# Gated linear attention and a bilinear feed-forward on one core: seven input loads move to ScalarE's own hardware queue, and seven filling matmuls run ahead of the first sums

## The chip, the cores and the metric

The kernel runs on one core of one Trainium2 chip. The metric is the device time of one execution in microseconds (us). Of each kernel there are a few timed runs and one profiled execution with its trace; times inside the kernel are counted from the start of the profiled span. The engines are called as the profile calls them: PE (matmuls; PEld loads its weights), DVE (VectorE), ACT (ScalarE), POOL (GpSimd) and SP (SyncE). A "q" behind a name (SPq, ACTq, PEq) is the sequencer of that engine, which issues DMAs and waits on semaphores.

## The reference, cut to what is computed

```
# q, k, v, alpha: (B, H, S, D) = (4, 8, 768, 48); moe_w_a, moe_w_b: (384, 1536); moe_w_out: (1536, 384)
for t in range(S):
    state = alpha[:, :, t, :, None] * state + einsum('bhd,bhe->bhde', k[:, :, t], v[:, :, t])
    y[:, :, t] = einsum('bhd,bhde->bhe', q[:, :, t], state)
x = y.transpose(0, 2, 1, 3).reshape(B * S, H * D)
out = ((x @ w_a) * (x @ w_b)) @ w_out
```

A recurrence with one decay per token, head and channel gives y; each token's eight heads side by side are a row of 384 numbers; and a feed-forward layer multiplies two projections to 1536 channels with each other and projects back to 384.

## The kernel before, in words

**Chunks.** The work is cut into six chunks. Chunk c holds 256 tokens (the third c // 2 of the sequence) of two of the four batches (c % 2 tells which two). Its loads `ld a`, `ld q`, `ld k`, `ld v` (function `load`, line 404) bring alpha, q, k and v of both batches into tiles of 128 partitions; each partition gets two neighbouring tokens of every head, so every contiguous run in HBM is 384 bytes. A load of a, q or k for a whole chunk is 768 KB of float32, one of v is cast to bfloat16 on its way. The tiles of a, q and k have two buffers each, so a load for chunk c can only start when the readers of chunk c - 2 are done.

**Attention of one chunk.** ACT takes logarithms of alpha (`ln`, line 411), PE sums them along the tokens (`B` line 453, `A2` line 503, `AQ` line 498), ACT makes exponentials of the sums (`E`, line 532: `beta` and `invb`). POOL or DVE multiplies one of the two tokens of each pair of q and k by a ratio, in place (`lv`, level, line 517; for q it reads `ra`, which ACT makes at line 510). DVE multiplies k by invb (`mk`) and q by beta (`mq`) into `QKp` (line 543). `QKp` is turned into `kqT`, in chunks 0 and 1 by PE, later by a DMA transpose that SP issues (`T`, line 595). PE makes scores (`D`, line 665), which are masked by DVE (`M`, line 670) or copied by ACT (`Mc`, line 674) and masked in place by DVE (`Mm`, line 678). `KA` and `K` (line 618) update the running state, `SA`, `SB` (line 694) and `Y` (line 715) add up y, `X` (lines 755 and 757) takes it out of PSUM on ACT or DVE, and `XT` (line 762) turns it by a DMA transpose that SP issues, into `xT`.

**Feed-forward of one chunk.** For each of the twelve blocks f of 128 channels PE computes `a f` and `b f` from xT (line 777, three matmuls each, of 512 tokens), ACT copies the a part out (`as f`, line 783), and DVE multiplies it with the b part into `prod` (`pr f`, line 791). Then `o m 0` and `o m 1` (line 799, six matmuls each, over f 0 to 5 and 6 to 11) project 128 tokens back; `ot` (lines 814, 816) copies the result out, and `st` (line 832) stores it.

**Order.** All of it stands in one hand-written list, `PROGRAM` (lines 17 to 258). An entry `3: ld k * P` means: of chunk 3, load k of both batches (`*`), issued from POOL (`P`; `S` is ACT, `V` is DVE, `Y` is SP). The number behind `a`, `b`, `D`, `o` and others is the PSUM bank, of eight. The list is walked once, and each engine executes its own instructions in the order of the list; engines wait for each other on semaphores only. So an engine that has little to do, such as POOL, gets ahead of the others in the list until one of its instructions has to wait. The attention of chunk c + 1 and c + 2 is woven between the feed-forward matmuls of chunk c.

**The places that the change touches.** At the head: `c1a` (line 325) loads ACT's table, `c1` (`const_fill`, line 327) sets on DVE the tile `wz` of zeros and two small constants, `fill n i` (line 435) runs n matmuls of wz with itself, 128 x 512, into bank i; their results are never read. Before the change, `c1` stands behind `Bs 0b`, and there are two fills: `fill 5 2` and `fill 1 1`. Along the way: the loads `4: ld a` (line 97), `3: ld k` (147), `4: ld q` (150), `5: ld a` (157), `4: ld k` (177), `5: ld k` (184) and `5: ld q` (215). Their first users:

- `3: ld k` is followed in its own entry by `lv 0 k P; lv 1 k P`; two entries on stand `mk 0 V; mq 0 V` of the same chunk, and then `2: a 1 * 2; b 5 * 0; as 5 *; pr 5 *`. A later `2: a 7 * 0` uses bank 0 again, which `pr 5` has to free.
- `5: ld a` is first read by `5: ln *` (line 166), behind which ACT has `as 11`, `ot 1`, `as 6` and `as 8` of the same stage; the `a 6 * 5` there uses the bank that `as 11` frees.
- `4: ld k` is followed at once by `lv 1 k V; lv 0 k V`, and DVE has `3: X 1 V` behind them (line 182), whose `XT 1` gives the last part of chunk 3's xT.
- `5: ld q` is followed by `lv 1 q P`; `lv 0 q V` (line 225) stands on DVE ahead of `3: pr 7` (line 226), which `3: o 2 1` needs.

Of the kernel before, what the change touches and what calls it, by code (L numbers as in the profile page):

```python
# [14 lines left out]


PROGRAM = """
0: c1a; cz 0 q V; cz 0 b P; cs 0 m P; ci; cz 1 q V; cz 0 v V; ld a 0b Y; ln 0b; cs 0 0 P; cm 0; cu; cu2 P; B 0b 3; Bs 0b; c1; cs 1 m P; ld v 0 P; ld a 1 P
0: cz 1 b P; ld a 0a Y; ln 0a; B 0a 1; Bs 0a; E 0a b; fill 5 2; cus; ld q 0a Y; mq 0a V; E 0b i; ld q 0b Y; ld k 0a Y; ld k 0b Y; mk 0b V; E 0b b; mq 0b V
0: C 0 1 5; E 0a i; mk 0a V; Ce 0 1 V; C 0 0 3; Ce 0 0 V; dk 0 6; fill 1 1; v 0 S; de 0; K 0 0 7; k 0 0 V; ln 1; cs 1 0 P; ld q 1 P; ld k 1 P; W b 0 256  # L20
0: cm 1; ld v 1 P; c2 P; c3 P; D 0 1 5; M 0 1; D 0 0 0; SB 0 6; B 1a 4; Bs 1a; Mc 0 0; Mm 0 0 V; B 1b 5; Bs 1b; E 1a i; E 1a b; mq 1a V; mk 1a V; K 0 1 4; E 1b i
# [72 lines left out]
1: pr 10 0; b 0 0 1; a 3 0 4; as 0 0; pr 0 0  # L94
2: lv 1 k P; mk 1 V
1: as 3 0; b 3 0 7; a 1 0 6; as 1 0
4: ld a * P
1: b 7 0 0; b 1 0 4; pr 1 0; as 7 0; pr 7 0; pr 3 0
2: mk 0 V
1: SB 1 0  # L100
3: ln *
1: a 6 0 2; as 6 0; b 9 0 3; a 4 0 5; a 9 0 6; as 9 0; pr 9 0
2: mq 1 V; T 1
0: o 2 0 4
# [39 lines left out]
2: a 5 * 6; b 4 * 3  # L144
3: E 1 i
1: st 0 Y
3: dr; ld k * P; lv 0 k P; lv 1 k P
4: lx V; R 0
3: mk 0 V; mq 0 V; T 0
4: ld q * Y  # L150
2: a 1 * 2; b 5 * 0; as 5 *; pr 5 *
4: ra 1
2: b 7 * 4; b 10 * 1; pr 4 *; a 10 * 6; as 10 *; pr 10 *
3: mk 1 V
2: a 7 * 0; b 1 * 5; a 0 * 6; b 0 * 7; as 1 *; as 7 *; pr 1 *; pr 7 *; as 0 *; a 3 * 0; b 9 * 1; pr 0 *
3: mq 1 V; ld v * P
5: ld a * P
2: as 3 *; b 3 * 2; a 9 * 6
4: ra 0
2: pr 3 *; as 9 *; pr 9 *; a 2 * 5  # L160
4: lv 0 q P
2: as 2 *; b 2 * 7; pr 2 *
3: KA * 06; D 0 0 4; M 0 0; dl; k * 0 V; k * 1 V
# [10 lines left out]
4: lv 1 q V  # L174
3: SB 1 4; D 1 1 0; Mc 1 1; Mm 1 1 V; SA 0; Y 0; X 0 S; XT 0
2: o 0 0 2
4: ld k * P; lv 1 k V; lv 0 k V
2: o 0 1 -
4: AQ 6; E 0 i
2: ot 0 S  # L180
4: E 0 b
3: SA 1; Y 1; X 1 V; XT 1
4: E 1 i; E 1 b; mk 1 V
5: ld k * P; lv 1 k P
2: o 2 0 1; o 2 1 -; o 3 0 6; o 1 0 0; o 3 1 -; o 1 1 -
4: dr
1: st 1 Y
# [24 lines left out]
4: SB 0 3; SB 1 5; D 1 1 0; Mc 1 1  # L212
3: b 3 * 7; pr 3 *; b 10 * 2
4: D 1 0 0; Mc 1 0; Mm 1 1 V
5: ld q * P; lv 1 q P
3: pr 10 *
4: SA 1; SA 0; Y 0; X 0 S; XT 0
3: o 2 0 7; o 1 0 1
# [737 lines left out]
```

## Time and profile before

| | us |
|---|---|
| median of 3 runs | 205.07 |
| lowest and highest of them | 195.19 and 207.42 |
| the profiled execution's own time | 196.55 |
| its span, first to last instruction | 194.8 |
| PE busy | 183.4 (94%) |
| DVE busy | 137.2 (70%) |
| ACT busy | 103.0 (53%) |
| POOL busy | 55.8 (29%) |

The span is the time from the first to the last instruction of the profiled execution; 1.75 us of its own time lie around it. Busy time of PE is that of overlapping matmuls, whose ends are modelled. The idle time of an engine counts only where another one waits for it in the end. The profile has a chain of waits: the work that ended last, followed back from the last instruction, at each step to whatever released it. A timeline row has the start, the time taken, the engine, the line, the operation, output and inputs, how many instructions were merged, and, in brackets, how long the engine had been idle and what ended that. For DMAs "to landing" is the time from the issue to the last byte's arrival.

### The profile page before, as it was taken

How to read it: one execution, taken by the hardware profiler on the slowest of the kernel's cores; microseconds unless marked ns; L12 is line 12 of the kernel's file. 1: busy time of each engine (PE TensorE's matmuls, PEld its weight loads, DVE VectorE, ACT ScalarE, POOL GpSimd, SP SyncE). 2: the span in 40 equal slices, each digit the busy share in tenths (PEclk: the TensorE clock that was granted, in tenths of full speed). 3: DMA queues.
4: the chain of work that ended last, by engine and by line, in shares of the span. 5: the costliest groups of instructions: out<-in, count | busy, mean ns of one | idle time of the engine just before them, and what ended most of it. 6: DMA issues, size and time to landing. Idle time of an engine off the chain costs nothing.

```text
span 194.8 us, 5851 instructions
## 1 busy us (share of the span) xinstructions
PE 183.4 (94%) x2498; PEld 111.5 (57%) x2498; DVE 137.2 (70%) x230; ACT 103.0 (53%) x189; POOL 55.8 (29%) x75
## 2 busy tenths in 40 slices
PE   1998899899999999999998989999999999999993
PEld 1577675566687877644555534555544556544463
DVE  3588966999899796779979379786755871147520
ACT  4465766686765668555566035766245712154401
POOL 8999734860640424400512400040000000000000
PEclk9999999999999999999999999999999999999999
DMA  5999999999999997999996996566388005013013
GB/s 127 263 214 188 237 231 257 245 247 258 255 228 232 189 252 142 127 267 226 131 237 131 131 277 150 111 51 78 82 156 183 3 3 112 9 43 121 2 40 122
DMA packets 57882, 30.96 MB, mean 159 GB/s; under 512 B 47824, under 2 KB 54880, under 8 KB 57856
## 3 DMA queue, kind: packets, MB, share of 16 engines
q0 software_dynamic: 19680, 18.09, 49.0%
q1 hardware_dynamic: 38032, 12.41, 31.5%
q8 instruction: 19, 0.31, 0.6%
q10 hardware_dynamic: 144, 0.10, 0.2%
q14 instruction: 7, 0.06, 0.1%
HBM read 25.98 MB, written 4.74 MB: 158 GB/s over the span
## 4 chain that ended last, share of the span: by engine, by line
PE 75%; DMA 10%; POOL 8%; issue 2%; DVE 2%; ACT 2%; POOLq 0%; ACTq 0%; DVEq 0%
PE psum L777 43%; PE psum L799 20%; DMA wb_t<-in_moe_w_b_dram 7%; DMA xT<-ys 3%; PE psum L665 3%; PE psum L715 2%; PE psum L618 2%; DVE prod L791 1%; POOL a_t L404 1%; PE psum L498 1%; PE psum L689 1%; PE psum L694 1%; POOL wa_t L384 1%; PE psum L810 1%; POOL v_t L404 1%
## 5 line engine op out<-in xcount | busy, mean ns | idle before, releaser
L777 PE MATMUL psum<-xT,wb_t 128*128 128x512 bf16 (+1 forms) x270 | 57.1, 337 | 0.8 <-DVE prod L791 0.3
L777 PE MATMUL psum<-xT,wa_t 128*128 128x512 bf16 (+1 forms) x270 | 56.1, 337 | 0.7 <-DMA xT<-ys 0.7
L799 PE MATMUL psum<-wo_t,prod 128*128 128x384 bf16 x276 | 48.5, 326 | 0.7 <-issue 0.7
L777 PEld LDWEIGHTS <-wb_t 128*128 128x128 bf16 x270 | 25.6, 98 | 21.6 <-issue 1.1
L777 PEld LDWEIGHTS <-wa_t 128*128 128x128 bf16 x270 | 25.4, 98 | 20.5 <-issue 1.2
L799 PEld LDWEIGHTS <-prod 128*128 128x128 bf16 x276 | 26.2, 98 | 17.6 <-issue 0.7
L517 POOL TENSOR_TENSOR q_t<-q_t,ra 128x384 f32<-128x384 f32 x8 | 9.1, 1135 | 46.8 <-ACT ra L510 32.0
L674 ACT ACTIVATE m<-psum 128x1024 bf16<-128x1024 f32 x16 | 16.2, 1022 | 6.3 <-PE psum L665 6.3
L816 DVE COPY ot<-psum 128x384 f32<-128x384 f32 (+1 forms) x13 | 6.9, 538 | 16.5 <-PE psum L799 14.1
L814 ACT ACTIVATE ot<-psum 128x384 f32<-128x384 f32 (+1 forms) x12 | 5.7, 477 | 12.9 <-PE psum L799 11.9
L678 DVE TENSOR_TENSOR m<-m,mask 128x1024 bf16<-128x1024 bf16 x16 | 11.6, 732 | 0.4 <-ACT m L674 0.4
L543 DVE TENSOR_TENSOR QKp<-k_t,invb 128x768 bf16<-128x768 f32 x10 | 11.1, 1114 | 0.2
L411 ACT ACTIVATE la<-a_t 128x1536 f32<-128x1536 f32 (+2 forms) x9 | 9.5, 1057 | 3.2 <-DMA a_t<-in_alpha_dram 3.1
L670 DVE TENSOR_TENSOR m<-psum,mask 128x1024 bf16<-128x1024 f32 x8 | 9.7, 1218 | 1.6 <-PE psum L665 1.5
L543 DVE TENSOR_TENSOR QKp<-q_t,beta 128x768 bf16<-128x768 f32 x10 | 9.3, 946 | 0.0
L517 POOL TENSOR_TENSOR k_t<-k_t,a_t 128x384 f32<-128x384 f32 x5 | 4.9, 992 | 14.8 <-DMA k_t<-in_k_dram 14.8
L404 POOL DMA_DIRECT2D a_t<-in_alpha_dram x7 | 7.4, 1059 | 5.5 <-DVE prod L791 2.9
L665 PE MATMUL psum<-kqT 64*64 64x128 bf16 x384 | 8.6, 218 | 0.5 <-DVE prod L791 0.2
L453 PE MATMUL psum<-la,ut 128*128 128x192 f32 x16 | 4.7, 448 | 4.2 <-ACT la L411 4.2
L404 POOL DMA_DIRECT2D v_t<-in_v_dram x8 | 8.5, 1066 | 0.1
L665 PEld LDWEIGHTS <-kqT 64*64 64x64 bf16 x384 | 6.4, 107 | 2.9 <-issue 2.5
L755 ACT ACTIVATE ys<-psum 128x768 bf16<-128x768 f32 x7 | 5.6, 809 | 4.3 <-PE psum L694 2.3
(271 smaller groups left out, 274.6 us busy)
## 6 DMA issues: line engine op xcount, KB each, us to landing
out_dram<-ot SPq DMA_DIRECT2D x23, 192.0 KB, 2.6
a_t<-in_alpha_dram POOLq DMA_DIRECT2D x4, 768.0 KB, 11.4
k_t<-in_k_dram POOLq DMA_DIRECT2D x4, 768.0 KB, 8.2
q_t<-in_q_dram POOLq DMA_DIRECT2D x3, 768.0 KB, 10.3
v_t<-in_v_dram POOLq DMA_DIRECT2D x4, 384.0 KB, 6.2
a_t<-in_alpha_dram POOLq DMA_DIRECT2D x3, 384.0 KB, 5.6
q_t<-in_q_dram POOLq DMA_DIRECT2D x3, 384.0 KB, 14.1
k_t<-in_k_dram POOLq DMA_DIRECT2D x3, 384.0 KB, 14.0
```

Source lines behind the costliest of these rows:

```text
L404: eng.dma_start(out=t[:, us, hs].rearrange("p b h r d -> p (b h) (r d)"), in_=src[ch.b0 + us.start:ch.b0 + us.stop, hs, ch.s * 2 * C:(ch.s ...
L411: nc.scalar.activation(out=ch.la[:, us, hs].rearrange("p b h r d -> p (b h r d)"), in_=ch.a[:, us, hs].rearrange("p b h r d -> p (b h r d) ...
L517: eng.tensor_mul(x, x, by)
L543: eng.tensor_mul(QKp[ch.c % 2][:, u, j, :, hs, :D], src[:, u, hs].rearrange("p h r d -> p r h d"), f)
L665: nc.tensor.matmul(s2[g * HC:(g + 1) * HC, r, p, rk, :], lhsT=ch.kqT[u][rs, 1, rk, 2 * h + p, g * HC:(g + 1) * HC], rhs=queriesT(ch, u, 2 ...
L670: nc.vector.tensor_mul(m.rearrange("p r a k s -> p (r a) (k s)"), ch.s2[u, h].rearrange("p r a k s -> p (r a) (k s)"), maskn(4))
L674: nc.scalar.activation(out=m.rearrange("p r a k s -> p (r a) (k s)"), in_=ch.s2[u, h].rearrange("p r a k s -> p (r a) (k s)"), func=AF.Copy)
L678: eng.tensor_mul(x, x, maskn(4))
L777: nc.tensor.matmul(p, lhsT=(wa_t, wb_t)[w][:, kk, f * 128:(f + 1) * 128], rhs=ch.xT[:, us.start // 2:us.stop // 2, kk].rearrange("p u g s ...
L799: nc.tensor.matmul(op, lhsT=ch.prod[:, f, at:at + C], rhs=wo_t[:, f, :], start=(f == 0), stop=(f == NFF - 1))
L814: nc.scalar.activation(out=o_, in_=i_, func=AF.Copy)
L816: eng.tensor_copy(o_, i_)
```

## The change

Three things change, all of them in `PROGRAM`. First, `c1` moves to the very front and `fill 7 2` is added behind it, ahead of the first sums. Second, seven loads of 768 KB are issued from ACT (`S`): six that POOL issued and one (`4: ld q`) that SP issued. Third, two of the seven also move down the list: `4: ld a` from ahead of `1: b 7 0 0 ...` to behind `3: ln *`, and `5: ld a` from behind `3: ld v * P` to behind the entry with `pr 3`, `as 9` and `a 2`. Nothing else changes; no function is new.

```
@@ -15,7 +15,7 @@
 PROGRAM = """
-0: c1a; cz 0 q V; cz 0 b P; cs 0 m P; ci; cz 1 q V; cz 0 v V; ld a 0b Y; ln 0b; cs 0 0 P; cm 0; cu; cu2 P; B 0b 3; Bs 0b; c1; cs 1 m P; ld v 0 P; ld a 1 P
+0: c1a; c1; fill 7 2; cz 0 q V; cz 0 b P; cs 0 m P; ci; cz 1 q V; cz 0 v V; ld a 0b Y; ln 0b; cs 0 0 P; cm 0; cu; cu2 P; B 0b 3; Bs 0b; cs 1 m P; ld v 0 P; ld a 1 P
 0: cz 1 b P; ld a 0a Y; ln 0a; B 0a 1; Bs 0a; E 0a b; fill 5 2; cus; ld q 0a Y; mq 0a V; E 0b i; ld q 0b Y; ld k 0a Y; ld k 0b Y; mk 0b V; E 0b b; mq 0b V
...
@@ -94,11 +94,11 @@
-4: ld a * P
 1: b 7 0 0; b 1 0 4; pr 1 0; as 7 0; pr 7 0; pr 3 0
 2: mk 0 V
 1: SB 1 0
 3: ln *
+4: ld a * S
 1: a 6 0 2; as 6 0; b 9 0 3; a 4 0 5; a 9 0 6; as 9 0; pr 9 0
...
@@ -144,20 +144,20 @@
 2: a 5 * 6; b 4 * 3
 3: E 1 i
 1: st 0 Y
-3: dr; ld k * P; lv 0 k P; lv 1 k P
+3: dr; ld k * S; lv 0 k P; lv 1 k P
 4: lx V; R 0
 3: mk 0 V; mq 0 V; T 0
-4: ld q * Y
+4: ld q * S
 2: a 1 * 2; b 5 * 0; as 5 *; pr 5 *
 4: ra 1
 2: b 7 * 4; b 10 * 1; pr 4 *; a 10 * 6; as 10 *; pr 10 *
 3: mk 1 V
 2: a 7 * 0; b 1 * 5; a 0 * 6; b 0 * 7; as 1 *; as 7 *; pr 1 *; pr 7 *; as 0 *; a 3 * 0; b 9 * 1; pr 0 *
 3: mq 1 V; ld v * P
-5: ld a * P
 2: as 3 *; b 3 * 2; a 9 * 6
 4: ra 0
 2: pr 3 *; as 9 *; pr 9 *; a 2 * 5
+5: ld a * S
 4: lv 0 q P
 2: as 2 *; b 2 * 7; pr 2 *
 3: KA * 06; D 0 0 4; M 0 0; dl; k * 0 V; k * 1 V
 1: o 1 0 2
 2: b 11 * 7
 5: ln *
 2: a 11 * 5; as 11 *; pr 11 *
...
@@ -174,14 +174,14 @@
 3: SB 1 4; D 1 1 0; Mc 1 1; Mm 1 1 V; SA 0; Y 0; X 0 S; XT 0
 2: o 0 0 2
-4: ld k * P; lv 1 k V; lv 0 k V
+4: ld k * S; lv 1 k V; lv 0 k V
 2: o 0 1 -
 4: AQ 6; E 0 i
 2: ot 0 S
 4: E 0 b
 3: SA 1; Y 1; X 1 V; XT 1
 4: E 1 i; E 1 b; mk 1 V
-5: ld k * P; lv 1 k P
+5: ld k * S; lv 1 k P
...
@@ -212,7 +212,7 @@
 4: SB 0 3; SB 1 5; D 1 1 0; Mc 1 1
 3: b 3 * 7; pr 3 *; b 10 * 2
 4: D 1 0 0; Mc 1 0; Mm 1 1 V
-5: ld q * P; lv 1 q P
+5: ld q * S; lv 1 q P
 3: pr 10 *
```

## The prediction on record

> **What bounds the kernel now.** I read the page first, then PE's own waits, then the chain of waits, then the loads and the rows around each of them.
>
> ```profile
> PE 183.4 (94%) x2498; PEld 111.5 (57%) x2498; DVE 137.2 (70%) x230; ACT 103.0 (53%) x189; POOL 55.8 (29%) x75
> ```
>
> PE is busy for 94% of a span of 194.8 us; POOL, which issues most loads, for 29%. The view of waits, for PE alone, says what PE lacks (waiter, releaser, total us, times, longest):
>
> ```profile
> PE psum L453 <- ACT la L411: 4.2, 1, 4.2
> PE psum L799 <- issue: 0.7, 1, 0.7
> PE psum L777 <- DMA xT<-ys: 0.7, 1, 0.7
> ```
>
> One wait of 4.2 us at the head, then nothing over 0.7 us. No row of that view names a load of q, k, v or alpha: behind the head PE never stands still for the transfers that are moved. So there is little to win on them, and whatever makes one late is paid in full, because PE has no slack to swallow it. In the chain of waits one transfer is long:
>
> ```profile
> 17.14 13.55 DMA wb_t<-in_moe_w_b_dram
> ```
>
> The last piece of w_b, issued by POOL at 17.14, lands at 30.69, and the next step is PE's. Up to there the kernel goes at the pace of POOL's issues and of the weight loads, and the change touches neither.
>
> **The head.** DVE and PE:
>
> ```profile
> 0.93 1.03 DVE L366 MEMSET QKp<- 128x512 f32 x2 [0.93 <-PEq L940]
> ```
> ```profile
> 4.19 2.90 PE L453 MATMUL psum<-la,ut 128*128 128x192 f32 x8 [4.19 <-ACT la L411]
> 6.88 2.15 PE L437 MATMUL psum<-wz 128*128 128x512 bf16 x5
> ...
> 12.71 1.76 PE L453 MATMUL psum<-la,ut 128*128 128x192 f32 x8
> ```
>
> DVE can zero wz from 0.93 on, so the new fills start at about 1.2; seven at 2.15 / 5 = 0.43 us take 3.0 us and end at 4.2, just where the first sum starts now. They are covered by that 4.2 us wait, with nothing to spare: a start 0.5 us later would delay the sums by as much. In return PE is awake earlier. The same eight sums take 2.90 us cold and 1.76 us later, so 1.1 us is the most the first sums gain. But all of this lies ahead of 30.69, where the weights are awaited. I take 0; ends -1.1 and +0.5 us. Moving `c1` costs nothing: DVE idles from 2.8 us until those sums.
>
> **What the loads cost in general.** Six issues of 0.9 to 1.2 us leave POOL, nearly 7 us, for which PE never waits: 0. Seven come to ACT. What one costs there is read from SP, the only engine here that issues such a load to a hardware queue:
>
> ```profile
> L404 SPq DMA_DIRECT2D q_t<-in_q_dram x3: 473/507/508, 1.8 to 88.3; - x3
> ```
> ```profile
> q_t<-in_q_dram SPq DMA_DIRECT2D x1, 768.0 KB, 6.3
> ...
> a_t<-in_alpha_dram SPq DMA_DIRECT2D x2, 192.0 KB, 2.8
> ```
> ```profile
> GB/s 127 263 214 188 237 231 257 245 247 258 255 228 232 189 252 142 127 267 226 131 237 131 131 277 150 111 51 78 82 156 183 3 3 112 9 43 121 2 40 122
> ```
> ```profile
> L404 POOL DMA_DIRECT2D k_t<-in_k_dram x2: 1148/1169/1190, 95.8 to 97.0; - x2
> DMA to landing us min/median/max: 6.6/7.7/8.9
> ```
>
> So 0.47 us of issue and x = 6.3 us to landing, the same size on the same kind of queue with transposes around it; this I take. The low end is 4.9: a 192 KB load takes 2.8 with the DMA engines nearly empty, and at the page's best slice, 277 GB/s, the other 590 KB take 2.1. The high end is 8.9, the slower of two POOL loads back to back.
>
> What decides is *when* ACT reaches the load. POOL ran ahead of the list; ACT keeps step with PE, since it copies out PE's results. That gives four places.
>
> **A, k of chunk 3** (line 147).
>
> ```profile
> 68.27 1.20 POOL L404 DMA_DIRECT2D k_t<-in_k_dram  x1
> 75.92 1.94 POOL L517 TENSOR_TENSOR k_t<-k_t,a_t 128x384 f32<-128x384 f32 x2 [6.45 <-DMA k_t<-in_k_dram]
> ```
> ```profile
> 82.59 0.60 ACT L783 ACTIVATE as__1760<-psum 128x512 bf16<-128x512 f32 x1 [0.16 <-PE psum L777]
> ```
> ```profile
> 83.33 0.95 DVE L543 TENSOR_TENSOR QKp<-k_t,invb 128x768 bf16<-128x768 f32 x1
> 84.19 0.95 DVE L543 TENSOR_TENSOR QKp<-q_t,beta 128x768 bf16<-128x768 f32 x1
> 85.25 0.73 DVE L791 TENSOR_TENSOR prod<-as__1796,psum 128x512 bf16<-128x512 bf16 x1
> ```
> ```profile
> 84.33 2.11 PE L777 MATMUL psum<-xT,wb_t 128*128 128x512 bf16 x9
> 86.27 1.03 PE L777 MATMUL psum<-xT,wa_t 128*128 128x512 bf16 x4
> ```
>
> POOL issued it at 68.27. On ACT it stands behind `as 4` (the row at 82.59, which waits for PE) and two exponentials, so it goes out at 82.6 and lands at 88.9. POOL's first multiply of k takes half of 1.94: 89.9. DVE's `mk 0`, at 83.33 now, waits 6.5 us, and `mq 0` and `pr 5` stand behind it in DVE's order; `pr 5` ends at 85.98 + 6.5 = 92.5. PE needs it for `a 7`, the fourth matmul of the last row: 86.27 + 3 x 0.216 = 86.9 (0.216 is the step of the nine ahead). PE stands for 5.6 us; in general A = x - 0.7. The load `4: ld q` goes out right behind it, in the same queue; its first user, POOL's `lv 0 q`, comes behind the late multiplies: 0. Both issues delay `as 5` by 1 us, and a full queue by more, under the same wait: 0. POOL now holds `3: ld v` behind the late multiplies: out at about 91, some 6.5 us to land, and its user `KA` comes at 93.5 + 5.6 = 99.1: covered, with 1.5 us left. `T 0` on SP is late by the same 6.5, and is used much later.
>
> **B, alpha of chunk 5** (moved down).
>
> ```profile
> 92.30 0.60 ACT L783 ACTIVATE as__1858<-psum 128x512 bf16<-128x512 f32 x1 [0.93 <-PE psum L777]
> ...
> 93.44 1.48 ACT L411 ACTIVATE la<-a_t 128x1536 f32<-128x1536 f32 x1
> 96.83 0.60 ACT L783 ACTIVATE as__1975<-psum 128x512 bf16<-128x512 f32 x1 [1.92 <-PE psum L777]
> ```
> ```profile
> L411 ACTq EVENT_SEMAPHORE  x1: 17/17/17, 93.0 to 93.0; - x1
> ```
> ```profile
> 97.61 0.59 PE L777 MATMUL psum<-xT,wa_t 128*128 128x512 bf16 x2
> ```
>
> All places in the old time, each stall by itself. The load goes out when `as 9` is released, 92.3, and one copy later ACT wants it for `ln`: landing at 98.6, logarithm 1.48, `as 11` 0.60, end 100.7. PE's `a 6` needs that bank at 97.61: 3.1 us, B = x - 3.2. Queued behind the waiting `ln` on ACT are `as 11`, `ot 1`, `as 6` and `as 8`; PE waits for the first of them, the others follow it.
>
> **C, k of chunk 4** (line 177).
>
> ```profile
> 102.61 0.81 ACT L755 ACTIVATE ys<-psum 128x768 bf16<-128x768 f32 x1
> ```
> ```profile
> 104.50 1.01 DVE L517 TENSOR_TENSOR k_t<-k_t,a_t 128x384 f32<-128x384 f32 x2
> ```
> ```profile
> 106.61 6.22 DMA xT<-ys
> ```
> ```profile
> DMA to landing us min/median/max: 2.8/3.1/3.8
> ```
>
> It goes out behind `X 0`, whose own wait is over at about 102.3 (it starts only when the copy ahead ends), and lands at 108.6; DVE's `lv 1 k` is due at 104.50. So DVE is 4.1 us late, with it `X 1` and the transpose `XT 1` that PE awaits: issued at 110.7 instead of 106.61. There is some room: by the chain that transpose took 6.22 us, while the seven whose landing the trace shows took 2.8 to 3.8. With 3.8 it lands at 114.5 instead of 112.8: C = 1.6, or x - 4.7; with 6.2 again, 4.1. I take 3.8, because the load of v that went out beside it (106.9) is now later, behind POOL's `lv 1 k`. The k of chunk 5 leaves ACT at 105.0 and is used by DVE only 12 us later: 0.
>
> **D, q of chunk 5** (line 215).
>
> ```profile
> 130.89 1.02 ACT L674 ACTIVATE m<-psum 128x1024 bf16<-128x1024 f32 x1 [0.52 <-PE psum L665]
> ```
> ```profile
> 133.42 0.55 DVE L517 TENSOR_TENSOR q_t<-q_t,ra 128x384 f32<-128x384 f32 x1
> 135.65 0.73 DVE L791 TENSOR_TENSOR prod<-as__2470,psum 128x512 bf16<-128x512 bf16 x1 [1.68 <-PE psum L777]
> ```
> ```profile
> 135.54 3.90 PE psum L799 x24
> ```
>
> Out at 130.9, there at 137.2; DVE's `lv 0 q` is due at 133.42, and `pr 7` stands behind it: 137.2 + 0.55 + 0.73 = 138.5. PE needs `pr 7` at the eighth of these 24 matmuls: 135.54 + 7 x 0.163 = 136.7. D = 1.8, or x - 4.5.
>
> **The rest: 0.** `4: ld a` goes out behind `3: ln`, some 15 us ahead of its use; its 0.47 us on ACT may push a copy, 0 to 0.5.
>
> **The sum.** A 5.6 + B 3.1 + C 1.6 + D 1.8 = 12.1 us. The profiled execution took 196.55 us (span 194.8, with 1.75 around it): 208.7. That execution is 1.4 above the lowest run (195.19) and 8.5 below the median (205.07), so runs of the changed kernel may lie apart by as much. Bounds: with x = 4.9 the stalls are 4.2 + 1.7 + 0.2 + 0.4 = 6.5, and with the head's best 5.4: 202.0. With x = 8.9 they are 8.2 + 5.7 + 4.2 + 4.4 = 22.5: 219; C's slower transpose would add 2.4 at most.
>
> **Rivals.**
>
> *The ACT queue lets a load pass (not slower).* If a load on ACT does not wait for the copies ahead of it, it goes out earlier. A has to end with x - 0.7 less the lead, and so on; at 2.5 us of lead the sum is 3.1 + 0.6 = 3.7, under 2%. With a lead of eight instructions k of chunk 3 would go out at about 79, A = 2, and the rest is covered: 198.5. Against it stands the ACTq row in B: the semaphore wait that belongs to `ln` is for a load that had long landed, and was still taken at 93.0 (92.95), when the copy ahead of it started, not before; so waits on ACT are taken in order, and a load whose buffer has to come free waits for semaphores in the same stream. The Trainium skill, "Advanced Engine Details and Errata", section Sequencer and Instruction Queues, speaks for it: engine instructions go into a queue (by its Engine Queue Depths eight deep on ScalarE) and the sequencer executes other instructions itself. No run here yet shows a load on ACT amid copies. Chance 0.13, of it 0.04 that the head's gain and a quicker transpose make it faster.
>
> *The clock falls in the long stall (slower still).* PE starts cold: from 4.19 to 9.03 its steps are twice as long, five fills 0.43 us against 0.216 later. If 5.6 us of standing in A sends it back there, another 4.8 us at half speed lose 2.4: 211; in B as well, 213.5. The trace of before has no stall that could show it. The Trainium skill, "TensorE: Matmul & The Clock Gate", section What's actually happening, has the clock halved after an idle window of about 3.4 us that runs freely, so by it A would meet one more often than not and B not; the head agrees with its waking time. Chance 0.25.
>
> *The loads are fast (x near 4.9).* ACT's queue is empty and the loads in A have little beside them: 203. Against it: 6.3 was measured on just such a queue. Chance 0.12, still slower.
>
> **How the numbers follow.** Forecast, 0.50: 208.7, own range 205 to 213. Clock 0.25, fast loads 0.12, passing 0.13. Over 2% slower: 0.50 + 0.25 + 0.12 = 0.87; within 2% (about what a measurement of this kernel can tell from no change) 0.09; faster 0.04. The range from 201 to 220 leaves out the passing case and the extremes of x, and takes in runs as far apart as those of before.
>
> **What would show it.** Some 5.6 MB on ACT's hardware queue, taken from POOL's (4.7) and SP's (0.8). PE waiting at L777 for DVE `prod` L791, once for 5 to 6 us; ACT `ln` L411 waiting for alpha for some 5 us; DVE L517 waiting for k and q for 4 us each. Load issues on ACT close behind the release of the copy ahead. I am wrong if those issues stand well ahead of it, if PE shows no idle time over 2 us, or if the loads land in under 4 us.

## The result, and the profile after

| | before | after |
|---|---|---|
| median of the runs, us | 200.34 (4 runs) | 212.72 (4 runs) |
| lowest and highest, us | 195.19 and 207.42 | 211.22 and 213.85 |
| the profiled execution, us | 196.55 | 211.98 |
| its span, us | 194.8 | 210.2 |

The change makes the kernel slower: 1.088 times the time before, with a 95% interval from 1.075 to 1.102. Runs of the kernel before lie between 195 and 207 us, and every ratio in this document is taken against those of them that are within 1.5% of its lowest. So 8.8% are some 17 us over 195.4; the two profiled executions are 15.4 us apart, the two medians 12.4. Forecast were 208.7 us, 12.1 over the profiled execution of before, in a range from 201 to 220.

The page of the kernel after: the busy row, the clock granted to TensorE in 40 slices, and the DMA queues (packets, MB, share): q0 is POOL's, q1 is SP's, q10 is ACT's.

```profile
PE 188.3 (90%) x2505; PEld 112.9 (54%) x2505; DVE 137.5 (65%) x230; ACT 103.4 (49%) x189; POOL 48.5 (23%) x69
...
PEclk9969999999999999958997999999999999999999
...
q0 software_dynamic: 18432, 13.37, 36.8%
q1 hardware_dynamic: 35968, 11.62, 27.1%
q10 hardware_dynamic: 14592, 5.60, 11.6%
```

PE is busy for 90% of a longer span, POOL is 7 us less busy for nothing, and 5.60 MB go over ACT's queue (5.5 MB more than before; POOL's carried 18.09 and SP's 12.41). New are the dips of the clock in the second row: one at the head (half clock from 10.83 to 14.25 us), after which PE still reaches the weights awaited at 30.7 us no later than before, and two in the middle. PE's waits of the kernel after (waiter, releaser, total us, times, longest), and then its chain of waits:

```profile
PE psum L777 <- DVE prod L791: 6.0, 1, 6.0
PE psum L777 <- ACT as__1982 L783: 4.8, 1, 4.8
...
PE psum L777 <- DMA xT<-ys: 2.3, 1, 2.3
...
PE psum L799 <- DVE prod L791: 0.8, 1, 0.8
```
```profile
82.25 6.05 DMA k_t<-in_k_dram
...
92.75 5.08 PE psum L777 x15
...
99.86 8.12 DMA a_t<-in_alpha_dram
...
110.08 2.72 PE psum L777 x6
...
116.67 5.29 DMA k_t<-in_k_dram
...
127.73 9.22 PE psum L777 x42
...
145.13 5.28 DMA q_t<-in_q_dram
...
154.62 11.01 PE psum L777 x51
```

Where the kernel before had no wait of PE over 0.7 us behind the head, it has four now, and they are the four places A, B, C and D: 6.0 us behind `pr 5`, 4.8 behind `as 11`, 2.3 behind the transposed x, 0.8 behind `pr 7`. Each is led by one of the moved loads, and the chain shows the landing time of each: 6.05, 8.12, 5.29 and 5.28 us.

The chain of the kernel before has the same two groups of matmuls at

```profile
112.96 9.22 PE psum L777 x42
...
139.44 11.01 PE psum L777 x51
```

so the delay can be read off where it arises. The matmul that needs `pr 5` starts at 92.75 instead of 86.92 (86.27 + 3 x 0.216): 5.8 us late. `a 6` starts at 110.08 instead of 97.61: 12.5 late. The group of 42 starts at 127.73 instead of 112.96: 14.8. The group of 51: 15.2, and that stays to the end. Between A and B 6.6 us are added, but the stall of B is 4.8; between B and C 2.3. The rest is the clock. The view of windows, cut at the clock's own steps, has these stretches (busy us and count of PE, PEld, DVE, ACT, POOL; then granted clock, DMA share and GB/s):

```profile
85.92:89.34 3.42, 0.82 (x4) 0.29 (x3) 0.00 (x0) 0.66 (x2) 0.91 (x1) 1.00 1.20 301
89.34:92.75 3.41, 0.00 (x1) 0.00 (x1) 3.29 (x4) 0.02 (x1) 2.17 (x3) 0.50 0.51 87
92.75:96.17 3.42, 3.42 (x9) 1.22 (x9) 2.59 (x4) 1.17 (x2) 0.00 (x0) 0.50 1.63 141
...
106.40:109.82 3.42, 0.00 (x0) 0.00 (x0) 0.00 (x0) 1.76 (x2) 0.00 (x0) 1.00 0.02 2
109.82:113.23 3.41, 3.15 (x34) 1.20 (x37) 0.73 (x1) 1.52 (x4) 0.00 (x0) 0.50 0.00 0
```

PE works from 92.75 to 96.17 at half clock (3.42 us, so 1.7 lost) and from 110.08 to 113.23 (3.15 us, so 1.6 lost): 3.3 us in all. The delays then split into A 5.8, clock 1.7, B 4.9, clock 1.6, C 0.7, D 0.4: 15.1 of the 15.4 us by which the profiled execution is longer. (Of D's stall of 0.8 us only 0.4 are left as delay.)

### The profile page after: what moved, and what is told of

The parts are those of the page before. It is cut to its first block, busy times and chain, and to the rows that moved or that the text cites. A ratio compares the mean times of both kernels' runs of the same rounds, so it can differ in the third digit from the quotient of the medians.

```text
span 210.2 us, 5868 instructions
## 1 busy us (share of the span) xinstructions
PE 188.3 (90%) x2505; PEld 112.9 (54%) x2505; DVE 137.5 (65%) x230; ACT 103.4 (49%) x189; POOL 48.5 (23%) x69
## 4 chain that ended last, share of the span: by engine, by line
PE 70%; DMA 16%; DVE 4%; issue 3%; ACT 3%; SPq 1%; POOL 1%; DVEq 0%; ACTq 0%; POOLq 0%
PE psum L777 40%; PE psum L799 16%; DMA k_t<-in_k_dram 8%; DMA a_t<-in_alpha_dram 4%; PE psum L665 3%; DMA q_t<-in_q_dram 3%; PE psum L689 2%; PE psum L618 2%; DMA xT<-ys 2%; PE psum L584 2%; DVE prod L791 1%; DVE QKp L543 1%; SPq L404 1%; PE psum L694 1%; PE psum L810 1%
## 5 line engine op out<-in xcount | busy, mean ns | idle before, releaser
L777 PE MATMUL psum<-xT,wa_t 128*128 128x512 bf16 (+1 forms) x270 | 58.6, 347 | 13.2 <-DVE prod L791 6.0
L777 PE MATMUL psum<-xT,wb_t 128*128 128x512 bf16 (+1 forms) x270 | 57.7, 339 | 0.0
L799 PE MATMUL psum<-wo_t,prod 128*128 128x384 bf16 x276 | 48.8, 326 | 0.8 <-DVE prod L791 0.8
L777 PEld LDWEIGHTS <-wa_t 128*128 128x128 bf16 x270 | 26.0, 99 | 34.7 <-issue 16.6
L799 PEld LDWEIGHTS <-prod 128*128 128x128 bf16 x276 | 26.0, 98 | 18.2 <-DVE prod L791 1.5
L517 POOL TENSOR_TENSOR q_t<-q_t,ra 128x384 f32<-128x384 f32 x8 | 8.6, 1080 | 48.1 <-ACT ra L510 26.9
L517 POOL TENSOR_TENSOR k_t<-k_t,a_t 128x384 f32<-128x384 f32 x5 | 5.4, 1084 | 47.9 <-DMA k_t<-in_k_dram 47.8
L678 DVE TENSOR_TENSOR m<-m,mask 128x1024 bf16<-128x1024 bf16 x16 | 10.8, 683 | 0.3 <-ACT m L674 0.2
L665 PE MATMUL psum<-kqT 64*64 64x128 bf16 x384 | 9.2, 228 | 0.2 <-DVE kqT L592 0.2
L404 POOL DMA_DIRECT2D v_t<-in_v_dram x8 | 8.6, 1074 | 0.1
L584 PE MATMUL psum<-ident,QKp 128*128 128x128 bf16 x64 | 5.1, 220 | 2.5 <-DVE QKp L543 2.4
L618 PEld LDWEIGHTS <-QKp 64*64 64x64 bf16 x320 | 4.7, 110 | 3.2 <-issue 2.6
## 6 DMA issues: line engine op xcount, KB each, us to landing
q_t<-in_q_dram POOLq DMA_DIRECT2D x2, 768.0 KB, 12.4
```

The lines of the kernel that those rows point to most:

```text
L404: eng.dma_start(out=t[:, us, hs].rearrange("p b h r d -> p (b h) (r d)"), in_=src[ch.b0 + us.start:ch.b0 + us.stop, hs, ch.s * 2 * C:(ch.s ...
L517: eng.tensor_mul(x, x, by)
L584: nc.tensor.transpose(t[:, j, r, p], QKp[ch.c % 2][:, u, j, r, hp:hp + 2, :].rearrange("s h d -> s (h d)"), ident)
L618: nc.tensor.matmul(kv[r * DP:(r + 1) * DP, e:e + D], lhsT=QKp[ch.c % 2][gs, u, 1, rk, 2 * p + r, :], rhs=value(ch, gs, u, rk, 2 * p + r), ...
L665: nc.tensor.matmul(s2[g * HC:(g + 1) * HC, r, p, rk, :], lhsT=ch.kqT[u][rs, 1, rk, 2 * h + p, g * HC:(g + 1) * HC], rhs=queriesT(ch, u, 2 ...
L678: eng.tensor_mul(x, x, maskn(4))
```

## The experiments

**Theory and rivals.** The theory to be tested: the time goes into loads that ACT issues too late, into the half clock behind the stalls, and, for B, into a load that meets SP's transposes. Rivals: the seven filling matmuls do something; loads on ACT's hardware queue cost time wherever they stand; the 8.1 us of alpha come from the number of loads.

**The head alone, and the loads alone.** `e1_head` is the kernel before with

```
-... Bs 0b; c1; cs 1 m P; ...
+0: c1a; c1; fill 7 2; cz 0 q V; ... Bs 0b; cs 1 m P; ...
```

and `e2_loads` is the kernel after with these two edits undone.

> The kernel before with the head of the change alone (the constants and seven fills at the front, no load moved). Theory 'late loads': the whole loss of 15 us comes from the loads, so this is the time of before within 0.5%, with PE's wait of 1.9 us behind the fills and the clock's dip near 11 us as in the changed kernel, both ahead of the weight load that PE awaits at about 30.7 us. Rival 'head': the dip of the clock at the head costs 1 us or more at the end, 197.5 or over where before takes 196.

> The changed kernel without its head (seven loads on ACT, constants and fills as before). Theory 'late loads': the time of the changed kernel within 0.5%, some 212 us, with PE's stalls of about 6, 4.8, 2.3 and 0.8 us in the same places. Rival 'head': 1 us or more below it.

Measured: 201.26 us for the head alone, 1.010 times [0.996, 1.025], which can't be told from no change; 212.16 for the loads alone, 1.084 [1.069, 1.098], as the whole change. So the loads are the loss, as far as it can be measured. That the head by itself is free is not shown: its two shortest runs, 198.23 and 198.31 us, lie above the 197.5 of the rival 'head', beside 195.59 and 196.89 for the kernel before. In the kernel after the first eight sums do run faster,

```profile
4.17 1.54 PE L453 MATMUL psum<-la,ut 128*128 128x192 f32 x8
...
8.71 1.56 PE L584 MATMUL psum<-ident,QKp 128*128 128x128 bf16 x16 [1.92 <-DVE QKp L543]
```

1.54 us instead of 2.90, and PE then waits for DVE's product instead (1.92 us ahead of 8.71). The matmuls that waited for the last piece of w_b start at 30.66 (30.74 before), now behind PE's own work and not behind that load. In the trace of `e1_head` they start at 31.73: there the clock is at half from 12 to 15.5 us.

**The same loads, early.** `e3_early` leaves all seven loads on ACT's queue and puts six of them far up the list, where their buffers are already free (`3: ld k` ahead of chunk 3's `lv 1 q`, `4: ld q` behind `4: ln *`, and so on).

```
-3: dr; ld k * S; lv 0 k P; lv 1 k P
+3: dr; lv 0 k P; lv 1 k P
-3: ra 1; lv 1 q P
+3: ra 1; ld k * S; lv 1 q P
...
```

> The changed kernel with the same seven loads on the same ACT queue, but each put so far up the list that ACT reaches it about when POOL issued it before (k of chunk 3 behind the ratio of chunk 3 near 67 us, q of chunk 4 behind the logarithm of chunk 4 near 75, alpha of chunk 5 near 78, k of chunks 4 and 5 near 90 and 93, q of chunk 5 near 105). Theory 'late loads': all four stalls of PE are gone and the time is that of before within 1%, some 196. Rival 'queue': what costs is the hardware queue itself (384-byte packets beside SP's transposes and POOL's loads, issues that hold ACT up for up to 2 us), so at least half of the 15 us stays, 203 or more.

Measured: 204.44 us, 1.041 [1.032, 1.050]. The theory's 196 us is missed, and the 203 from which the rival begins is passed. Over half of the 8.8% is gone, so lateness is a cause; but 4% stay, so it isn't the only one. The longest of PE's waits, and the page's row of DMA issues for the transposed x (count, median us to landing), say what is left:

```profile
PE psum L666 <- DMA kqT<-QKp: 2.1, 1, 2.1
```
```profile
xT<-ys SPq DMA_TRANSPOSE x8, 6.3
```

The longest wait of PE is now for one of SP's transposes, issued at 96.91, between ACT's loads of k of chunk 4 (95.27) and chunk 5 (97.84); it takes 9.49 us to land. That of x takes 6.3 us to land in the median, where the kernel before had 3.1. The loads themselves are early; they make other transfers late. In this trace, too, a step of half clock (74.74 to 78.15) follows a wait of PE.

**The clock by itself.** `e4_warm` is the kernel after with filling matmuls, whose results nobody reads, put into the two long stalls:

```
-2: a 7 * 0; b 1 * 5; ...
+2: fill 22 5; a 7 * 0; b 1 * 5; ...
-2: a 6 * 5; as 6 *; a 8 * 3; as 8 *
+2: fill 17 3; a 6 * 5; as 6 *; a 8 * 3; as 8 *
```

> The changed kernel with 22 fills ahead of the matmul that waits 6.0 us (place A) and 17 ahead of the one that waits 4.8 us (place B), into banks that are free; PE then works on zeros while it waits, and each fill takes 0.216 us, so they end before the wait does. Theory 'the clock adds to the stalls': granted clock 1.0 through both places, and 1.7 + 1.6 = 3.3 us less than the changed kernel, some 208.7 where that takes 212. Rival 'the stalls are all': the same time as the changed kernel within 0.5%.

Measured: 209.67 us, 1.070 [1.055, 1.085]: by the medians 3.05 us less than the kernel after and 2.5 less than `e2_loads`, run in the same round. Both stretches behind the stalls are now at full clock (93 to 100 and 100 to 112):

```profile
93.00:100.00 7.00, 7.00 (x111) 3.52 (x110) 6.31 (x10) 3.10 (x6) 1.02 (x1) 1.00 1.24 164
100.00:112.00 12.00, 10.90 (x172) 5.59 (x170) 6.08 (x10) 5.01 (x7) 0.00 (x0) 1.00 0.52 81
```

The loads are as late as before (6.15 and 8.08 us to landing), and only the clock changes. From A's matmul to B's it now takes 15.61 us instead of 17.33, from B's to C's 16.16 instead of 17.65: 1.7 and 1.5 us, 3.2 together, are the clock's share. That the medians give nearly the same is in part chance, since this execution reached A 0.9 us earlier and lost 1.7 us to half clock in another place (last section).

**One load at a time.** Each of four kernels is the kernel before with one of the loads moved as in the change: k of chunk 3 (`e5_a`), alpha of chunk 5 (`e6_b`), k of chunk 4 (`e7_c`), q of chunk 5 (`e8_d`).

```
e5_a  -3: dr; ld k * P; lv 0 k P; lv 1 k P      +3: dr; ld k * S; lv 0 k P; lv 1 k P
e6_b  -5: ld a * P   (line 157)                 +5: ld a * S   (behind the entry with pr 3, as 9, a 2)
e7_c  -4: ld k * P; lv 1 k V; lv 0 k V          +4: ld k * S; lv 1 k V; lv 0 k V
e8_d  -5: ld q * P; lv 1 q P                    +5: ld q * S; lv 1 q P
```

> The kernel before with only k of chunk 3 moved to ACT (place A). Theory 'late loads': PE stands for 6 us at the a matmul behind pr 5, the clock is at half for two of its windows and 1.7 us go there; and POOL, which still issues alpha of chunk 5 and now holds it behind the late multiplies, brings that about 13 us later than before, which may add 0 to 2. In all 7.5 to 9.5 us over before. Rival 'queue': 3 us or less, since one load on the queue has little to contend with.

> The kernel before with only alpha of chunk 5 moved down the list and to ACT (place B). Theory 'late loads': ACT's logarithm waits for the whole load, x - 3.2 us of it reach PE: 3.1 us if the load takes 6.3, 4.9 if it takes 8.1 as in the changed kernel, and 0 to 1.6 for the clock. 3 to 6.5 us over before. Rival 'queue': it took 8.1 there only because of the loads put on the queue before it, so 3 us or less here.

> The kernel before with only k of chunk 4 moved to ACT (place C). Theory 'late loads': DVE stands for some 3 to 4 us at its first multiply of that k, and PE for 1.6 to 2.3 us at xT; no dip of the clock. 1.0 to 2.5 us over before. Rival 'queue': nothing that can be measured.

> The kernel before with only q of chunk 5 moved to ACT (place D). Theory 'late loads': the load takes 5.3 us as in the changed kernel, DVE stands for about 3 us and PE for 0.8 at pr 7. 0.4 to 1.0 us over before, hard to tell from nothing. What counts is the trace: PE idle ahead of L799 by DVE prod. Rival 'queue': no such idle time.

Measured: 208.73 us, 1.060 [1.041, 1.079]; 203.59, 1.037 [1.032, 1.042]; 203.46, 1.036 [1.020, 1.052]; 197.88, 1.005 [0.992, 1.019]. By the ratios, on 196.4 us, that is about +12, +7, +7 and +1. Their sum of some 27 us is over one and a half times what the whole change costs (8.8%, some 17 us): the parts do not add. The first three cost more than expected.

A alone missed by 2 us or more. Its stall is as expected, 6.1 us. The chain of waits has more behind it:

```profile
98.08 1.04 SPq L404
...
101.57 5.08 DMA bl<-row
```

SP issues the load of q of chunk 4 here (L404), which the change takes off SP, and it now stands between the late `T 0` and the small decay rows that the state update needs (`bl`, which land 5.08 us after their issue). The kernel after, where `4: ld q` is ACT's, has no such wait; a kernel with these two moves alone was not run. Alpha of chunk 5, which POOL issues 12.5 us later here (91.43), was the cause that was expected; its share is open.

B alone costs slightly more than expected. Its stall is 5.0 us, behind `as 11`, with a single load on the queue:

```profile
92.45 0.45 ACTq L404 DMA_DIRECT2D a_t<-in_alpha_dram  x1
...
100.86 1.48 ACT L411 ACTIVATE la<-a_t 128x1536 f32<-128x1536 f32 x1 [7.22 <-DMA a_t<-in_alpha_dram]
```
```profile
92.17 2.82 SPq L595 DMA_TRANSPOSE kqT<-QKp  x1
```

It went out 0.28 us behind SP's transpose `T 1` and landed over 8 us later. So the number of loads on ACT's queue is not the cause. POOL's load of k moves beside it, though (0.59 MB from 95.1 to 100.8 us), so this kernel doesn't tell whether it waited for the transpose; `e9_b_up` below does.

C alone missed by 4 us or more: PE waits 7.0 us for the transposed x instead of 2.3 in the kernel after. The three stretches 109.4 to 112.5, 112.5 to 115.2 and 115.2 to 118.5 of this kernel have these rows for SP's queue (packets, MB, share of the 16 engines); then its chain:

```profile
q1 hardware_dynamic: 265, 0.06, 34.0%
...
q1 hardware_dynamic: 29, 0.01, 11.2%
...
q1 hardware_dynamic: 1068, 0.43, 104.8%
```
```profile
109.39 9.06 DMA xT<-ys
```

`XT 1` was issued at 109.39, when the load of v of chunk 4 (issued by POOL at 102.43, 12.7 us to landing) was still under way. SP's queue hardly moves until that load has landed at 115.1, and PE goes on at 118.58. POOL's load of q of chunk 5, issued right behind it (103.62), is under way as well. In the kernel after, v of chunk 4 is later (128.21), out of the way. `e10_v_early` and `e11_c_v` below test this.

D alone can't be told from no change in time. Its trace has the stall: PE waits 1.2 us for DVE's `prod` ahead of L799, where the kernel before has no such wait.

**v out of the transposes' way.** `e10_v_early` is the kernel before with

```
 5: ld a * P
+4: ld v * P
...
-4: ld v * P; K * 0 2; T 0; D 0 1 5
+4: K * 0 2; T 0; D 0 1 5
...
 4: T 1
+5: ld q * Y
...
-5: ld q * P; lv 1 q P
+5: lv 1 q P
```

so it moves the load of q of chunk 5 as well, and `e11_c_v` is `e7_c` with the first two of these edits, which move v alone.

> The kernel before, with no load on ScalarE's queue; v of chunk 4 is loaded by GpSimd earlier, behind alpha of chunk 5, and q of chunk 5 goes from GpSimd to SP. Theory: in the kernel before, the transposed x of chunk 3 is held up by the load of v of chunk 4, which moves beside it; apart from it the transposes land in 3 to 4 us, TensorE's wait for them is under 0.5 us, and every run takes about 195 us, with a spread of under 3 us. Rival, the wait has another cause: time and spread as before (about 195 to 207 us).

> k of chunk 4 alone on ScalarE's queue, and v of chunk 4 loaded early by GpSimd. Theory: the 7.0 us for which TensorE waited for the transposed x with k of chunk 4 alone moved came from the load of v beside the transposes; then the wait falls to 1.5 to 2.5 us, with no half clock, and the time is 1.5 to 2.5 us over that of v early without the moved load. Rival, the wait comes from the load of k itself: it stays near 7 us, and the time about 7 us above.

Measured: 199.18 us (197.89 to 200.48), 1.017 [1.010, 1.024], beside 201.11 (195.22 to 205.04) for the kernel before on the same chip; and 199.17 (198.73 to 199.82), 1.017 [1.011, 1.023]. The wait is explained: with k of chunk 4 on ACT's queue and v out of the way, PE waits 1.3 us for the transposed x instead of 7.0, and the transpose lands in 3.56 us instead of 9.06. POOL's load of q of chunk 5 still goes out 5.2 us ahead of it (105.99; 5.8 us in `e7_c`), so that load alone doesn't do it.

```profile
PE psum L778 <- DMA xT<-ys: 1.3, 1, 1.3
```
```profile
111.20 3.56 DMA xT<-ys
```

So the rival (the load of k itself) falls, and moving k of chunk 4 costs nothing measurable then (expected were 1.5 to 2.5 us). In `e10_v_early` the expected 195 us were missed: the spread of 10 us shrinks to under 3, but the floor rises by 2.7. The early load of v is now under way beside SP's `T 0`, which holds SP for 4.49 us (from 84.85) instead of 2.95, so the decay rows behind it go out later,

```profile
92.75 5.05 DMA bl<-row
```
```profile
PE psum L696 <- DVE prod L793: 1.6, 1, 1.6
```

at 92.75 instead of 91.2. They land in 5.05 us, no slower than before (5.5 in the median), and PE waits 1.6 us. This version is steadier than the kernel before; faster it is only against the median of all runs, and not against the lowest.

**Alpha ahead of the transposes.** `e9_b_up` is the kernel after with `5: ld a * S` one ACT copy earlier (behind `4: ra 0`).

```
 4: ra 0
+5: ld a * S
 2: pr 3 *; as 9 *; pr 9 *; a 2 * 5
-5: ld a * S
```

> All as in the changed kernel, only that the load of alpha of chunk 5 stands one ACT copy earlier, so that it goes out at about 97.9 us, ahead of the transposes that SP issues at 98.9 us. Theory: the load took 8.1 us because its packets waited behind those transposes; then it takes 5.5 to 6 us here and lands near 103.5, TensorE's wait for the exponentials of alpha falls from 4.8 to under 1 us, the half clock behind it goes, and the time falls by about 5.5 us against the changed kernel (some 206.5 to 207 us on its chip). Rival, the load takes 8 us wherever it stands: it lands near 106, the wait is about 2.9 us, and the time falls by 1.9 to 3.5 us (209 to 210 us).

Measured: 1.060 [1.050, 1.069], three runs of 206.63 to 208.01 us (one more of 646.59 is left out), 5 to 6 us under the kernel after. The load took 5.4 us, and the wait for `as 11` is gone from the view; of the four places A is now first and C second:

```profile
PE psum L777 <- DVE prod L791: 6.0, 1, 6.0
PE psum L777 <- DMA xT<-ys: 2.2, 1, 2.2
```
```profile
98.77 0.38 ACTq L404 DMA_DIRECT2D a_t<-in_alpha_dram  x1
...
104.24 1.48 ACT L411 ACTIVATE la<-a_t 128x1536 f32<-128x1536 f32 x1 [2.34 <-DMA a_t<-in_alpha_dram]
```
```profile
99.48 4.43 SPq L595 DMA_TRANSPOSE kqT<-QKp  x1
```

It goes out 0.7 us ahead of SP's `T 1` (99.48) and doesn't wait. For the kernel after, the queues in 99.9 to 102.4 and in 102.4 to 108 show the other order:

```profile
q1 hardware_dynamic: 1739, 0.45, 98.6%
...
q10 hardware_dynamic: 2064, 0.79, 67.2%
```

In the first 2.5 us all 1739 packets are SP's, and not one of the load's 2064 has begun: it was issued at 99.86, behind `T 1` (98.91), and stood behind it. The rival, 8 us wherever it stands, falls.

**All seven loads, clear of the transposes.** `e12_clear` is the kernel after with six of the loads moved to gaps that SP's transposes leave in the trace of the kernel before (the places that they are taken from are left out here).

```
 2: SB 1 3; D 0 1 1; Mc 0 1; Mm 0 1 V; k * 1 V
+3: ld k * S
...
 1: ... ot 3 S; st 3 Y
+5: ld a * S
...
 2: ... pr 4 *; a 10 * 6; as 10 *; pr 10 *
+4: ld q * S
...
 2: a 11 * 5; as 11 *; pr 11 *
+4: ld k * S
 1: o 1 1 -; ot 1 S
 2: a 6 * 5; as 6 *; a 8 * 3; as 8 *
+5: ld k * S
...
 5: ra 1
+5: ld q * S
```

> The same seven loads on ScalarE's queue and the same filling matmuls as in the changed kernel, each load put earlier, at a place where SP's transposes are not in flight by the trace of the kernel before. Theory, the loss is lateness of the loads plus their meeting with the transposes: within 1.5% of the kernel before (195 to 203 us), with no wait of TensorE over 2 us. Rival, loads on that queue cost some per cent wherever they stand: 203 us or more.

Measured: 198.41 us (198.34 to 198.99), 1.014 [1.008, 1.019]. Of the 8.8% that the change costs 1.4% are left, with the same loads on the same queue. The longest wait of PE:

```profile
PE psum L781 <- DMA xT<-ys: 1.9, 2, 1.6
```

No wait is over 2 us. The rival, that this queue costs some per cent in any place, falls. Against `e3_early`, which has the same loads early but among the transposes, the gain is 5 to 6 us. Not all of them are clear in this kernel's own trace (q of chunk 4 goes out at 86.94, behind a transpose of 84.86), and what makes up the last 1.4% is open.

## Why the prediction was wrong, and where it was right

**Right: the sign, the four places, and when the loads go out.** The forecast was over 2% slower, because ACT reaches the loads only when PE has released the copy ahead. ACT's rows of the kernel after:

```profile
82.24 0.60 ACT L783 ACTIVATE as__1767<-psum 128x512 bf16<-128x512 f32 x1 [0.16 <-PE psum L777]
82.25 0.37 ACTq L404 DMA_DIRECT2D k_t<-in_k_dram  x1
82.72 2.15 ACTq L404 DMA_DIRECT2D q_t<-in_q_dram  x1
82.74 0.48 ACT L532 ACTIVATE beta<-psum 128x384 f32<-128x384 f32 x1
```

The load goes out 0.01 us behind the start of the copy, and ahead of the exponentials that stand before it in the list but wait for nothing new. So the rival in which a load passes the waiting copies is out. The second load's issue took 2.15 us and pushed `as 5` to 84.97, under the same wait, as the prediction had allowed. POOL's 7 freed us were worth nothing, as predicted, and the head next to nothing: in these two traces PE is 0.35 us ahead when it comes to A (a row of 84.33 starts at 83.98).

**The sum of the stalls: right in total by luck, wrong in its parts.** With x = 6.3 us for every load the prediction had A 5.6, B 3.1, C 1.6, D 1.8: 12.1. The delays read off above are 5.8, 4.9, 0.7 and 0.4: 11.8. Its formulas agree to within half a microsecond when each load has its own landing time: A = 6.05 - 0.7 = 5.4, B = 8.1 - 3.2 = 4.9, C = 5.3 - 4.7 = 0.6, D = 5.3 - 4.5 = 0.8. So the step that took one x for four places was wrong by 1.8 us one way in B and by about 1 the other way in C and in D, and the errors cancel. That A agrees is chance in part: DVE's `mk 0` took 1.73 us instead of 0.95 while POOL still multiplied k, which the formula leaves out, and the head's 0.35 us pull the other way. B's load meets SP's `T 1`, which the prediction did not look for: it had named what stands behind the load on ACT, and not what stands on SP's queue at the time when the load goes out. `e9_b_up` shows it.

**The step that failed: the clock.** The prediction left it out of the sum and gave it 0.25, as a rival with 211 us for A alone and 213.5 with B. It is the case that came, in both, with 3.3 us by the windows and 3.2 by the trace of `e4_warm`: 208.7 + 3.3 = 212.0, where the profiled execution took 211.98. The rival priced each place at 2.4 us, from 4.8 us at half speed; PE worked at half clock for 3.42 and 3.15 us, so 1.7 and 1.6 are right. The mistake was double. For A, with 5.6 us of standing, the prediction itself said that the clock would fall more often than not, and still counted it at nothing. For B it took a stall of 3.1 us, which the load's real 8.1 us made 4.8.

The Trainium skill, "TensorE: Matmul & The Clock Gate", section What's actually happening, has half clock as the state after at least one idle window of about 3.4 us that runs freely. The windows here agree in length (3.41 us) and in being on a grid that doesn't start with the stall. They differ on "idle": 0.82 us of work in 3.42 was already enough for half clock (85.92 to 89.34), and the last section shows more.

**Not foreseen:** how much hangs on the load of v of chunk 4, which holds up the transposed x. The prediction put the 6.22 us of that transpose down to this load, and took 3.8 because v would be later; that was right, and the 3.68 us in the chain after bear it out. What it didn't see is that the same meeting can lengthen a whole execution with no load moved. The profiled execution of `e1_head` took 205.1 us: POOL issues v at 107.80 and q of chunk 5 at 108.98, the transpose issued at 109.17 takes 10.08 us, and PE waits 5.9 us for it:

```profile
PE psum L777 <- DMA xT<-ys: 7.3, 2, 5.9
```

The kernel before has the same loads in the same places, so this can happen to it as well. So the prediction was wrong in taking over the spread of the kernel before: it said that runs of the changed kernel may lie as far apart, and they lie within 2.6 us (211.22 to 213.85) instead of 12. That this explains all of the spread is not shown. `e10_v_early` moves the load of q of chunk 5 too, and `e8_d`, which takes only that load off POOL, has no run over 199.5 us either.

## What to carry to other kernels

A load belongs on a queue whose issuing engine reaches it early enough, so ask for each moved load when its new engine gets there, and what other transfers are under way at that moment: the same load took 5.4 us ahead of a transpose and 8.1 behind it. Price a stall of the bounding engine with its consequence: behind a stall of 4.8 us the half clock cost another 1.6 us. Where single edits add up to much more than they cost together, look for what each shifts into the way of another.

## What the runs showed of the hardware that was not expected

**A step that is half empty can be enough for half clock.** The granted clock changes in steps of 3.41 us, and a step at half follows a step in which PE was busy for too little. It need not be idle. Of `e4_warm`, and then of the kernel after, with a wait of PE for the transposed x in each (2.2 and 2.3 us):

```profile
120.48:123.89 3.41, 1.18 (x8) 0.51 (x7) 3.41 (x6) 0.00 (x0) 1.21 (x1) 1.00 0.78 156
123.89:127.30 3.41, 3.41 (x10) 1.18 (x9) 2.66 (x4) 1.08 (x2) 1.43 (x2) 0.50 0.43 78
```
```profile
123.48:126.89 3.41, 1.99 (x13) 0.98 (x10) 3.41 (x6) 0.00 (x0) 0.00 (x0) 1.00 1.16 172
126.89:130.31 3.42, 2.58 (x12) 1.20 (x13) 2.90 (x4) 1.09 (x3) 2.49 (x2) 1.00 0.71 162
```

In the first the wait falls inside one step, PE is busy for 1.18 of 3.41 us (35%), and the next step is at half clock: 1.7 us more. In the second the wait lies across a border, PE is busy for 58% and 75%, and nothing happens. So a stall of some 2 us can cost nearly twice its length, or not, by where it falls. Steps with 45% (`e5_a`, 1.55 of 3.42 us from 115.55) and 47% (`e3_early`, 1.61 of 3.44 from 71.30) are followed by half clock too. The busy share alone gives no border: at the head of the kernel after, a step with 57% (1.97 of 3.43 us from 7.40, much of it small matmuls) is followed by half clock as well. And the granted clock doesn't show the slow start: in the kernel before it reads 1.00 from 1.9 to 8.7 us, where five fills take 0.43 us each instead of 0.216.

**Transfers of different queues hold each other up, in these cases in the order of their issue.** A 768 KB load on ACT's queue waited for SP's transposes (8.1 instead of 5.4 us), loads early on ACT's queue doubled the landing time of the transposes (6.3 instead of 3.1 us), and POOL's load of v, beside them, made one take 9.06 instead of 3.56 us. That the queues share the 16 DMA engines would account for this; no run here tests it.
